# One two-bank transpose, a later channel mix and moved adds of x in a phase-mixing kernel on one Trainium2 core

## The chip, the cores and the metric

The kernel runs on one core of one Trainium2 chip. The metric is the device time in microseconds (us), and the median of several runs stands for a kernel. A single execution is also profiled: every instruction on every engine, every DMA transfer and the TensorE clock that was granted. TensorE multiplies matrices (PE in the profile; PEld is the loading of its weights), VectorE is DVE, ScalarE is ACT, GpSimd is POOL, and SP is the engine that issues most of the plain DMAs here.

## The reference

With B = 8, S = 4224, D = 192, the kernel computes a short causal convolution of x and then a token-mixing layer on the result:

```python
# convolution over 7 tokens, one softmax-normalised set of taps per head
out = np.einsum('hk,bskhg->bshg', w, x_unf)
x = out.reshape(B, S, D)
# mixing layer
theta = x @ w_theta
zr, zi = x * np.cos(theta), x * np.sin(theta)
y = np.einsum('ts,bsd->btd', w_tok_r, zr) + np.einsum('ts,bsd->btd', w_tok_i, zi)
u = x + y
return u + np.maximum(u @ w_ch, 0.0)
```

The two products with the 4224 x 4224 matrices w_tok_r and w_tok_i are nearly all of the arithmetic.

## The kernel before

**Tiling.** The source tokens are cut into 33 chunks of 128 (`NK`), the target tokens into 33 blocks of 128. All 8 batches lie side by side, so that a chunk of x is a tile of 128 tokens by 1536 values (`N`), in two halves of 768 (`GC`, four batches each). Only 11 chunks (`NW`) are held in SBUF at once. The work is a list of 58 steps (`NSTEP`). A step adds the contribution of the chunks that are held (up to 11) to two target blocks (`tbs`), so 17 steps (`NU`) go once round the targets, and each target block is visited three or four times. Between visits its partial sum `pv` lies in DRAM, in one of two arrays `part`: `load_rows` (line 356) fetches it one step ahead, and the end of `mix` (line 440) stores it.

**A step.** `mix` (line 414) computes a two-block step with seven runs of 2 x 11 matmuls of 384 columns (line 427) in place of eight, Strassen's scheme: some runs use sums of weight tiles. Each run ends with `give` (line 384), which adds its PSUM tile `y` into `pv`: on DVE (line 392), or on ACT in the first visit (line 390). The next step's weights are made while a step runs: `load_w` (line 307) fetches the raw rows on the POOL queue into `st`, `turn` (line 325) transposes them in 32 x 32 blocks on DVE (line 327), and `wsum` (line 333) forms the sums S1 to S4 on DVE (line 339, two fp16 inputs from SBUF).

**A chunk.** `Chunk` loads x (`xw`). `conv` makes the convolution (`pc`, line 200), evacuates it to the fp16 tile `x` and stores it in the DRAM array `xs`. `transpose` brings each half onto the other axis: six transposes into one bank of a PSUM tile `tp` (line 160), evacuated by `evacuate` to the tile `xT` (of the name `uT`; ACT line 148, DVE line 146). `theta` mixes the channels (`channel_mix`, PSUM tile `v`, line 138) and takes two sines on ACT (line 240), the first with a bias; `product` and `sums` (lines 245, 251) finish on DVE. The tiles `pc`, `tp` and `v` all come from `banks`: one pool of two buffers of two banks each. The first 11 chunks are made in the loop at the end of the program, where `between(n)` lets n pieces of the steps through; the other 22 are made inside steps 17 to 22 and 35 to 40.

**Adding x.** The sum u = x + y needs x in `pv`. `add_x` (line 368) does this once for each target block, in one of two ways. For 24 blocks it fetches x from `xs` into the one buffer `xr` and adds on POOL (line 374). For the 9 blocks of the last five steps (`late`) it lets a DMA on the POOL queue add `xs` into `part` in DRAM (line 379, two DMAs per block). That is four steps before they are needed, in steps 49 to 53.

**The output.** The last visit of a block (`final`, steps 41 to 57) ends with u. `cast` makes an fp16 copy `ub` on ACT (line 449); `cross_u` transposes it with a DMA through the crossbar, issued by ACT (line 155), in the 12 full final steps 41 to 52, and `turn_u` does so on PE in the last five; `output` mixes the channels (line 138 again), adds the relu to `pv` on DVE (line 464) and stores the result (line 469).

**Order.** `pe`, `dve`, `act` and `pool` chain the instructions of an engine in the order in which the program records them. That order is written by hand: each task of a step has a place between 0 and 7 (a run of matmuls is 1 unit, 3.6 us where 11 chunks are held), and `outputs` gives places in the list's own microseconds, 24.9 to a full step. An engine can start a recorded task as soon as its inputs are there, so a place binds PE, which is never far ahead, and is only an order for the others. The DMAs of SP are not chained; a scheduler orders them.

Of the kernel before, what the change touches and what calls it, by code (L numbers as in the profile page):

```python
# [9 lines left out]
AT = mybir.ActivationFunctionType  # L10
# [6 lines left out]
def kernel(  # L17
# [53 lines left out]
        mybir.DependencyClass.NoSync, mybir.DependencyReason.DATA  # L71
    )
# [84 lines left out]
    def transposed(uT, u, by_dve=False):  # L157
        tp = banks("tp", F16)
        for k in range(6):
            pe(nc.tensor.transpose(  # L160
                tp[:, 0, k * P : (k + 1) * P], u[:, k * P : (k + 1) * P], ident
            ))
        evacuate(uT.rearrange("p k s -> p (k s)"), tp[:, 0, 0 : 6 * P], by_dve)
# [3 lines left out]
    class Chunk:  # L167
# [53 lines left out]
        def transpose(self, g):  # L221
            if g == 0:
                self.xT = turned()
            transposed(
                self.xT[:, 6 * g : 6 * g + 6, :], self.x[:, g * GC : (g + 1) * GC],
                0 < self.k < 3 or (self.k, g) == (0, 1),
            )
# [27 lines left out]
        def tasks(self):  # L255

            for j in range(2):
                yield lambda j=j: self.conv(j)
            for g in range(NG):
                yield lambda g=g: self.transpose(g)  # L260
            for g in range(NG):
                yield lambda g=g: self.theta(g)
            yield lambda: self.product(Z11)
            yield lambda: self.product(Z21)
            yield lambda: self.sums(0)
            yield lambda: self.sums(1)
# [13 lines left out]
    class Step:  # L280


        def __init__(self, t):
            self.t, self.u, self.ks = t, unit(t), active(t)
            self.n = len(self.ks)
            self.tbs = [tb for tb in (2 * self.u, 2 * self.u + 1) if tb < NT]
            self.pair = len(self.tbs) == 2
            self.first = t < NU
            self.final = t + NU >= NSTEP
            self.late = self.final and self.n < NW  # L290
            self.ahead = self.late or 0 <= t + NU - NSTEP < 2
            visits = [v for v in range(NU, NSTEP) if v % NU == t % NU]
            self.adds = []
            for i, tb in enumerate(self.tbs):
                at = [v for v in visits if self.known(tb) < v - 1 and v + NU < NSTEP
                      and NU + 1 + base[-1] < v <= 2 * NU]
                at = at[0] if at else visits[-1]
                if t == at:
                    self.adds.append(i)
            self.time = 0.324 * self.n * (7 if self.pair else 4)  # L300
            self.st, self.w, self.ub, self.uT, self.pv = {}, {}, {}, {}, []
# [65 lines left out]

        def add_x(self, i):

            rows = slice(self.tbs[i] * P, (self.tbs[i] + 1) * P)  # L370
            if not self.ahead:
                xr = wk.tile([P, N], F16, name="xr", tag="xr", bufs=1)
                nc.sync.dma_start(out=xr, in_=xs[rows, :])
                pool(nc.gpsimd.tensor_tensor(  # L374
                    out=self.pv[i], in0=self.pv[i], in1=xr, op=ALU.add
                ))
                return
            for cols in (slice(0, HN), slice(HN, N)):
                pool(nc.gpsimd.dma_start(
                    out=part[(self.t // NU - 1) % 2][self.tbs[i], :, cols],  # L380
                    in_=xs[rows, cols], accum_op=ALU.add,
                ))
# [61 lines left out]
        def cast(self, i, g):  # L444
            if g == 0:
                self.ub[i] = wk.tile([P, N], F16, name="ub", tag="ub", bufs=2)
                self.uT[i] = turned()
            cols = slice(g * GC, (g + 1) * GC)
            act(nc.scalar.activation(  # L449
                out=self.ub[i][:, cols], in_=self.pv[i][:, cols], func=AT.Copy  # L450
            ))

        def turn_u(self, i, g):
            transposed(
                self.uT[i][:, 6 * g : 6 * g + 6, :], self.ub[i][:, g * GC : (g + 1) * GC]
            )
# [17 lines left out]
        def outputs(self):  # L474

            found = []
            for i in range(len(self.tbs)):
                if not self.late:
                    at = (4 if i else 0.9 - self.time / 7) if self.pair else 0.7
                    for g in range(NG):  # L480
                        found.append((at + g, lambda i=i, g=g: self.cast(i, g)))
                        found.append((at + 10.5 + 2.8 * g,
# [18 lines left out]
    def step_events(t):  # L501
        found = []
        s = steps[t]
        if t + 1 < NSTEP:
            found += steps[t + 1].w_tasks()
            found.append((1.6, steps[t + 1].load_rows))
            if not steps[t + 1].ahead:
                for i in steps[t + 1].adds:
                    found.append((3.3 + 1.7 * i, lambda i=i: steps[t + 1].add_x(i)))
        for s in steps[t:]:  # L510
            if s.ahead and t == s.t - (4 if s.late else 10):
                for i in s.adds:
                    found.append((3.3 + 1.7 * i, lambda s=s, i=i: s.add_x(i)))
# [8 lines left out]
        if t >= NU - 2:  # L522
# [4 lines left out]
            for k in (k for k in range(NK) if start[k] == t + 1 and k >= NW):  # L527
                pos = [0, .5, 1.3, 1.6, 2.1, 2.5, 3.1, 3.15, 3.4, 3.6]
# [116 lines left out]
    for i in range(NW + 2):  # L645
# [28 lines left out]
        if ch:  # L674
            ch.transpose(0)
        if old:
            old.product(Z11)
        between(1)
        if ch:
            ch.transpose(1)  # L680
# [9 lines left out]
    nc.vector.memset(wch[:, 1:3, :], 0.0)  # L690
# [36 lines left out]
```

## Time and profile before

| what | us |
| --- | --- |
| median of 13 runs | 1475.89 |
| fastest and slowest run | 1462.62, 1481.54 |
| the profiled execution, own time | 1477.95 |
| its span in the profile | 1476.2 |
| PE busy | 1425.0 (97%) |
| DVE busy | 1012.1 (69%) |
| ACT busy | 323.1 (22%) |
| POOL busy | 434.8 (29%) |

The profiled execution lies 2.1 us above the median, and 1.7 us of its time lie outside its span. PE's busy time says when it had a matmul in flight, not that it worked at its peak.

### The profile page before, as it was taken

The page shows a single profiled execution, that of the slowest core. Times are in us where ns is not written, and L with a number is a line of the kernel's source. Part 1 is how long each engine was busy: PE and PEld are TensorE (multiplying, and loading weights), DVE is VectorE, ACT ScalarE, POOL GpSimd, SP SyncE. Part 2 cuts the span into 40 slices and gives each one's busy share as a digit, 9 for nine tenths or more (in the row PEclk, how much of TensorE's full clock was granted, in tenths as well). Part 3 has the DMA queues.
Part 4 walks back from the last instruction along what each step waited for, and adds up shares of the span by engine and source line. Part 5 has one row for each costly group of instructions (what it writes and reads, how often), then busy time and mean ns, then how long its engine had stood idle before and what let it go on. Part 6 is the DMA issues. An engine that isn't in the chain of part 4 may idle for free.

```text
span 1476.2 us, 23773 instructions
## 1 busy us (share of the span) xinstructions
PE 1425.0 (97%) x9807; PEld 889.6 (60%) x9807; DVE 1012.1 (69%) x1050; ACT 323.1 (22%) x413; POOL 434.8 (29%) x655
## 2 busy tenths in 40 slices
PE   7889999999999999999999999999999999998997
PEld 4556666666666666666656566666666666555565
DVE  6884555545458687867767758768777786675575
ACT  6861111111134353000000005245001001000034
POOL 7422211111223322522413333332132133333210
PEclk9999999999999999999999999999999999999999
DMA  9976756464699999997978799999899989999983
GB/s 169 215 175 148 141 97 151 90 150 91 153 226 213 227 222 262 192 251 162 246 164 217 171 195 240 191 235 267 150 216 214 196 195 230 200 210 198 232 215 122
DMA packets 272028, 281.98 MB, mean 191 GB/s; under 512 B 106672, under 2 KB 240176, under 8 KB 271920
## 3 DMA queue, kind: packets, MB, share of 16 engines
q0 software_dynamic: 162464, 92.15, 48.3%
q1 hardware_dynamic: 71824, 178.88, 35.2%
q10 hardware_dynamic: 37632, 9.44, 4.2%
q8 instruction: 77, 1.26, 0.3%
q14 instruction: 31, 0.25, 0.1%
HBM read 245.49 MB, written 108.13 MB: 240 GB/s over the span
## 4 chain that ended last, share of the span: by engine, by line
PE 84%; DMA 6%; DVE 5%; ACT 3%; issue 1%; ACTq 0%; SPq 0%; DVEq 0%
PE y L427 75%; PE v L138 5%; DMA uT<-ub 4%; PE pc L200 2%; ACT z L240 1%; DVE wt L339 1%; DVE pv L392 1%; PE tp L160 1%; DMA pv<-part 1%; ACT uT L148 1%; DVE pv L464 1%; DVE wt L327 1%; DVE z L251 1%; DVE z L245 0%; DMA out_dram<-pv 0%
## 5 line engine op out<-in xcount | busy, mean ns | idle before, releaser
L427 PE MATMUL y<-z,wt 128*128 128x384 f16 x7656 | 1294.7, 327 | 11.7 <-DVE pv L392 10.8
L427 PEld LDWEIGHTS <-wt 128*128 128x128 f16 x7656 | 741.7, 98 | 489.6 <-issue 16.9
L392 DVE TENSOR_TENSOR pv<-y,pv 128x768 f32<-128x768 f32 x324 | 308.5, 953 | 310.5 <-PE y L427 271.2
L327 DVE STREAM_TRANSPOSE wt<-st 128x1408 f16<-128x1408 f16 (+7 forms) x224 | 327.6, 1465 | 41.5 <-PE y L427 36.2
L314 POOL DMA_DIRECT2D st<-in_moe_w_tok_i_dram x232 | 132.4, 579 | 500.7 <-DVE wt L327 485.3
L314 POOL DMA_DIRECT2D st<-in_moe_w_tok_r_dram x232 | 132.6, 580 | 460.4 <-DVE wt L327 447.1
L339 DVE TENSOR_TENSOR wt<-wt 128x1408 f16<-128x1408 f16 (+7 forms) x216 | 213.0, 986 | 45.6 <-PE y L427 43.4
L148 ACT ACTIVATE z<-pc 128x768 f16<-128x768 f32 x65 | 52.9, 813 | 389.4 <-PE pc L200 389.4
L449 ACT ACTIVATE ub<-pv 128x768 f16<-128x768 f32 x66 | 52.5, 836 | 361.3 <-DVE pv L392 332.4
L390 ACT ACTIVATE pv<-y 128x768 f32<-128x768 f32 x66 | 53.7, 813 | 282.7 <-PE y L427 282.7
L138 PEld LDWEIGHTS <-uT 128*128 128x128 f16 x1056 | 91.5, 99 | 38.8 <-DMA uT<-ub 15.6
L464 DVE SCALAR_TENSOR_TENSOR pv<-v,pv 128x768 f32<-128x768 f32 x66 | 62.8, 954 | 35.9 <-PE v L138 33.9
L187 POOL DMA_DIRECT2D xw<-in_x_dram x132 | 76.1, 585 | 30.8 <-issue 9.8
L374 POOL TENSOR_TENSOR pv<-pv,xr 128x1536 f32<-128x1536 f32 x24 | 74.8, 3118 | 13.4 <-issue 9.7
L148 ACT ACTIVATE uT<-tp 128x768 f16<-128x768 f16 x79 | 63.0, 815 | 63.1 <-PE tp L160 62.2
L251 DVE TENSOR_TENSOR z<-z 128x768 f16<-128x768 f16 x132 | 73.4, 556 | 3.8
L138 PE MATMUL v<-wch,uT 128*128 128x192 f16 x528 | 55.3, 249 | 15.0 <-DMA uT<-ub 13.1
L240 ACT ACTIVATE z<-v,half_pi 128x768 f16<-128x768 f32 x66 | 59.6, 903 | 42.9 <-PE v L138 42.7
L245 DVE TENSOR_TENSOR z<-z 128x1536 f16<-128x1536 f16 x66 | 60.4, 950 | 9.9 <-ACT z L240 9.9
L138 PE MATMUL v<-wth,uT 128*128 128x192 f16 x528 | 55.0, 248 | 3.0 <-ACT z L240 2.9
L240 ACT ACTIVATE z<-v 128x768 f16<-128x768 f32 x66 | 53.2, 805 | 0.0
L160 PE MATMUL tp<-ident,z 128*128 128x128 f16 x396 | 33.3, 221 | 8.4 <-ACT z L240 7.9
(43 smaller groups left out, 149.4 us busy)
## 6 DMA issues: line engine op xcount, KB each, us to landing
part<-pv SPq DMA_DIRECT2D x79, 768.0 KB, 4.2
pv<-part SPq DMA_DIRECT2D x79, 768.0 KB, 5.9
out_dram<-pv SPq DMA_DIRECT2D x66, 384.0 KB, 5.2
st<-in_moe_w_tok_r_dram POOLq DMA_DIRECT2D x136, 176.0 KB, 5.4
st<-in_moe_w_tok_i_dram POOLq DMA_DIRECT2D x136, 176.0 KB, 4.9
xs<-z SPq DMA_DIRECT2D x132, 96.0 KB, 4.5
xw<-in_x_dram POOLq DMA_DIRECT2D x121, 96.0 KB, 6.1
xr<-xs SPq DMA_DIRECT2D x24, 384.0 KB, 4.6
```

The source lines that it names most:

```text
L138: pe(nc.tensor.matmul(v[:, k, b * D : (b + 1) * D], lhsT=tT[:, 3 * k + b + i, :], rhs=w[:, 2 * b + i, :], start=(i == 0), stop=(i == 1),))
L148: act(nc.scalar.activation(out=out, in_=in_, func=AT.Copy))
L187: nc.gpsimd.dma_start(out=self.xw[lo : lo + n, h, :, :], in_=x[:, t0 : t0 + n, :].rearrange("b s d -> s b d"),)
L240: act(nc.scalar.activation(**args))
L251: dve(nc.vector.tensor_tensor(out=z[:, o, :], in0=z[:, a, :], in1=z[:, b, :], op=ALU.subtract))
L314: pool(nc.gpsimd.dma_start(out=st[a * Q : (a + 1) * Q, 0:nb, :, 0:n] .rearrange("i r bt s -> i (r bt) s"), in_=w[self.tbs[0] * P : (self.t ...
L327: dve(nc.vector.transpose(self.w[name][:, 0 : self.n, :, :], self.st[int(name[1])][:, int(name[0]) - 1, :, 0 : self.n * Q] .rearrange("p b ...
L339: dve(nc.vector.tensor_tensor(out=self.w[name][:, 0 : self.n, :, :], in0=self.w[a][:, 0 : self.n, :, :], in1=self.w[b][:, 0 : self.n, :, : ...
L374: pool(nc.gpsimd.tensor_tensor(out=self.pv[i], in0=self.pv[i], in1=xr, op=ALU.add))
L392: dve(nc.vector.tensor_tensor(out=o, in0=yv, in1=o, op=ALU.add))
L427: pe(nc.tensor.matmul(y[cn][:, q, 0:BH], lhsT=self.w[wn][:, c, :, :].rearrange("p bt i -> p (bt i)"), rhs=chunks[k].z[:, zn, q * BH : (q + ...
L464: dve(nc.vector.scalar_tensor_tensor(out=ub, in0=channel_mix(self.uT[i][:, 6 * g : 6 * g + 6, :], wch), scalar=0.0, in1=ub, op0=ALU.max, o ...
```

## The change

The diff has six edits.

1. `transposed` takes a list of halves. For x both halves go into the two banks of one PSUM tile, and one instruction evacuates 1536 columns. The first three chunks are evacuated by DVE, the rest by ACT. In the loop of the first chunks the 12 transposes stand together, ahead of the first product; in steps 17 to 22 and 35 to 40 the places of transposes and thetas move by about 0.1 unit.
2. In the full final steps `output` moves from the places 7.8, 10.6, 14.5, 17.3 (in the list's microseconds after the step's end) to 12, 14.7, 17.5, 20.2. The casts and the crossbar transfer of the second block move from 4, 5, 6 to 1, 2, 3.
3. The adds in DRAM for the last five steps move from steps 49 to 53 to steps 27, 29 and 31 (five blocks, in the other array `part`, one visit earlier) and step 41 (four blocks).
4. The fetch of `xr` is a task of its own (places 2 and 4). The POOL add moves from 3.3 and 5.0 to 3.6 and 5.6, and gets a wait: it starts after the DVE instruction recorded last before it has finished.
5. In the last two steps the first half of each cast is done by DVE instead of ACT.
6. The clearing of two slices of `wch` is chained in DVE's order.

```diff
@@ -70,6 +70,9 @@
     NOSYNC = mybir.DependencyInfo(
         mybir.DependencyClass.NoSync, mybir.DependencyReason.DATA
     )
+    SYNC = mybir.DependencyInfo(
+        mybir.DependencyClass.Sync, mybir.DependencyReason.SCHED_ONLY
+    )
     last = {}
 
     def in_order(engine, ins):
@@ -154,13 +157,20 @@
 
         act(nc.scalar.dma_start(out=uT, in_=u, transpose=True))
 
-    def transposed(uT, u, by_dve=False):
+    def transposed(uT, u, gs, by_dve=False):
+
         tp = banks("tp", F16)
-        for k in range(6):
-            pe(nc.tensor.transpose(
-                tp[:, 0, k * P : (k + 1) * P], u[:, k * P : (k + 1) * P], ident
-            ))
-        evacuate(uT.rearrange("p k s -> p (k s)"), tp[:, 0, 0 : 6 * P], by_dve)
+        for g in gs:
+            for k in range(6):
+                pe(nc.tensor.transpose(
+                    tp[:, g, k * P : (k + 1) * P],
+                    u[:, g * GC + k * P : g * GC + (k + 1) * P], ident,
+                ))
+        g = slice(gs[0], gs[-1] + 1)
+        evacuate(
+            uT[:, :, :].rearrange("p (g k) s -> p g (k s)", g=NG)[:, g, :],
+            tp[:, g, 0 : 6 * P], by_dve,
+        )
 
     Z11, T1, Z21, Z22, T2, T4, T3 = range(7)
 
@@ -218,13 +228,9 @@
                         out=xs[t0 : t0 + Q, :], in_=self.x[a * Q : (a + 1) * Q, :]
                     )
 
-        def transpose(self, g):
-            if g == 0:
-                self.xT = turned()
-            transposed(
-                self.xT[:, 6 * g : 6 * g + 6, :], self.x[:, g * GC : (g + 1) * GC],
-                0 < self.k < 3 or (self.k, g) == (0, 1),
-            )
+        def transpose(self):
+            self.xT = turned()
+            transposed(self.xT, self.x, range(NG), self.k < 3)
 
         def theta(self, g):
             v = channel_mix(self.xT[:, 6 * g : 6 * g + 6, :], wth).rearrange(
@@ -256,8 +262,7 @@
 
             for j in range(2):
                 yield lambda j=j: self.conv(j)
-            for g in range(NG):
-                yield lambda g=g: self.transpose(g)
+            yield self.transpose
             for g in range(NG):
                 yield lambda g=g: self.theta(g)
             yield lambda: self.product(Z11)
@@ -288,17 +293,21 @@
             self.first = t < NU
             self.final = t + NU >= NSTEP
             self.late = self.final and self.n < NW
-            self.ahead = self.late or 0 <= t + NU - NSTEP < 2
             visits = [v for v in range(NU, NSTEP) if v % NU == t % NU]
-            self.adds = []
+            quiet = [v for v in visits if start[2 * NW - 1] < v <= 2 * NU]
+            self.adds, self.ahead = [], []
             for i, tb in enumerate(self.tbs):
-                at = [v for v in visits if self.known(tb) < v - 1 and v + NU < NSTEP
-                      and NU + 1 + base[-1] < v <= 2 * NU]
-                at = at[0] if at else visits[-1]
-                if t == at:
+                known = self.known(tb)
+                if t not in ([v for v in quiet if known < v - 1] or visits[-1:])[:1]:
+                    continue
+                if not self.late:
                     self.adds.append(i)
+                else:
+                    far = known <= start[2 * NW - 1]
+                    self.ahead.append((i, 2 * NU - NW + 2 * (t % NU) if far else start[-1],
+                                       (t // NU - 1 - far) % 2))
             self.time = 0.324 * self.n * (7 if self.pair else 4)
-            self.st, self.w, self.ub, self.uT, self.pv = {}, {}, {}, {}, []
+            self.st, self.w, self.xr, self.ub, self.uT, self.pv = {}, {}, {}, {}, {}, []
 
         def known(self, tb):
 
@@ -365,20 +374,27 @@
                     )
                 self.pv.append(pv)
 
+        def load_x(self, i):
+            self.xr[i] = wk.tile([P, N], F16, name="xr", tag="xr", bufs=1)
+            nc.sync.dma_start(
+                out=self.xr[i], in_=xs[self.tbs[i] * P : (self.tbs[i] + 1) * P, :]
+            )
+
         def add_x(self, i):
 
-            rows = slice(self.tbs[i] * P, (self.tbs[i] + 1) * P)
-            if not self.ahead:
-                xr = wk.tile([P, N], F16, name="xr", tag="xr", bufs=1)
-                nc.sync.dma_start(out=xr, in_=xs[rows, :])
-                pool(nc.gpsimd.tensor_tensor(
-                    out=self.pv[i], in0=self.pv[i], in1=xr, op=ALU.add
-                ))
-                return
+
+            ins = pool(nc.gpsimd.tensor_tensor(
+                out=self.pv[i], in0=self.pv[i], in1=self.xr[i], op=ALU.add
+            ))
+            tc.add_manual_dep(ins.ins, last["dve"].ins.name, SYNC, reason="pace")
+
+        def add_ahead(self, i, which):
+
+            tb = self.tbs[i]
             for cols in (slice(0, HN), slice(HN, N)):
                 pool(nc.gpsimd.dma_start(
-                    out=part[(self.t // NU - 1) % 2][self.tbs[i], :, cols],
-                    in_=xs[rows, cols], accum_op=ALU.add,
+                    out=part[which][tb, :, cols], in_=xs[tb * P : (tb + 1) * P, cols],
+                    accum_op=ALU.add,
                 ))
 
         def give(self, y, i, h, copies):
@@ -446,14 +462,10 @@
                 self.ub[i] = wk.tile([P, N], F16, name="ub", tag="ub", bufs=2)
                 self.uT[i] = turned()
             cols = slice(g * GC, (g + 1) * GC)
-            act(nc.scalar.activation(
-                out=self.ub[i][:, cols], in_=self.pv[i][:, cols], func=AT.Copy
-            ))
+            evacuate(self.ub[i][:, cols], self.pv[i][:, cols], self.t >= NSTEP - 2 and g == 0)
 
         def turn_u(self, i, g):
-            transposed(
-                self.uT[i][:, 6 * g : 6 * g + 6, :], self.ub[i][:, g * GC : (g + 1) * GC]
-            )
+            transposed(self.uT[i], self.ub[i], [g])
 
         def cross_u(self, i):
             crossed(self.uT[i], self.ub[i])
@@ -476,10 +488,10 @@
             found = []
             for i in range(len(self.tbs)):
                 if not self.late:
-                    at = (4 if i else 0.9 - self.time / 7) if self.pair else 0.7
+                    at = 1 if i or not self.pair else 0.9 - self.time / 7
                     for g in range(NG):
                         found.append((at + g, lambda i=i, g=g: self.cast(i, g)))
-                        found.append((at + 10.5 + 2.8 * g,
+                        found.append((12 + 5.5 * i + 2.7 * g,
                                       lambda i=i, g=g: self.output(i, g)))
                     found.append((at + 2, lambda i=i: self.cross_u(i)))
                     continue
@@ -504,13 +516,12 @@
         if t + 1 < NSTEP:
             found += steps[t + 1].w_tasks()
             found.append((1.6, steps[t + 1].load_rows))
-            if not steps[t + 1].ahead:
-                for i in steps[t + 1].adds:
-                    found.append((3.3 + 1.7 * i, lambda i=i: steps[t + 1].add_x(i)))
-        for s in steps[t:]:
-            if s.ahead and t == s.t - (4 if s.late else 10):
-                for i in s.adds:
-                    found.append((3.3 + 1.7 * i, lambda s=s, i=i: s.add_x(i)))
+            for i in steps[t + 1].adds:
+                found.append((2 + 2 * i, lambda i=i: steps[t + 1].load_x(i)))
+                found.append((3.6 + 2 * i, lambda i=i: steps[t + 1].add_x(i)))
+        here = [(r, i, which) for r in steps for i, when, which in r.ahead if when == t]
+        for j, (r, i, which) in enumerate(here):
+            found.append((1.5 + 1.8 * j, lambda r=r, i=i, which=which: r.add_ahead(i, which)))
         if t + 2 < NSTEP:
             nxt = steps[t + 2]
             for m in (1, 2):
@@ -525,7 +536,7 @@
                 found.append((4.5, lambda k=k: load_chunk(k)))
             at = 0.1
             for k in (k for k in range(NK) if start[k] == t + 1 and k >= NW):
-                pos = [0, .5, 1.3, 1.6, 2.1, 2.5, 3.1, 3.15, 3.4, 3.6]
+                pos = [0, .5, 1.4, 2.2, 2.6, 3.1, 3.15, 3.4, 3.6]
 
                 def add(at, j, k):
                     def go():
@@ -672,12 +683,10 @@
             load_chunk(i + 3)
         between(1)
         if ch:
-            ch.transpose(0)
+            ch.transpose()
         if old:
             old.product(Z11)
-        between(1)
-        if ch:
-            ch.transpose(1)
+        between(2)
         if old:
             old.product(Z21)
         between(1)
@@ -687,7 +696,7 @@
         if old:
             old.sums(1)
         between(1)
-    nc.vector.memset(wch[:, 1:3, :], 0.0)
+    dve(nc.vector.memset(wch[:, 1:3, :], 0.0))
     for rows, i, part_w in channel_pieces(moe_w_ch):
         nc.gpsimd.dma_start(out=wch[rows, i, :], in_=part_w)
     ready[0] = NK
```

## The prediction

> **What bounds the kernel now.** I read the page first: its shares, its slices and the chain.
>
> ```profile
> span 1476.2 us, 23773 instructions
> PE 1425.0 (97%) x9807; PEld 889.6 (60%) x9807; DVE 1012.1 (69%) x1050; ACT 323.1 (22%) x413; POOL 434.8 (29%) x655
> ...
> PE 84%; DMA 6%; DVE 5%; ACT 3%; issue 1%; ACTq 0%; SPq 0%; DVEq 0%
> ```
>
> PE is the bound, and no edit here takes a matmul from it. What can be won is the time in which PE waits or runs slowly. So the next view is the list of waits, PE's rows alone:
>
> ```profile
> PE v L138 <- DMA uT<-ub: 13.1, 6, 3.1
> PE y L427 <- DVE pv L392: 10.8, 12, 1.8
> ...
> PE tp L160 <- ACT z L240: 7.9, 10, 1.1
> ```
>
> Each row has the total, the times and the longest. The first: the output's channel mix waits six times for the crossbar. The timeline shows where, here step 49's first block and, as a measure, the same 16 matmuls after a shorter wait:
>
> ```profile
> 1277.67 1.53 ACTq L155 DMA_TRANSPOSE uT<-ub  x1
> 1289.51 0.83 PE L138 MATMUL v<-wch,uT 128*128 128x192 f16 x8 [2.83 <-DMA uT<-ub]
> 1290.18 4.45 PE L427 MATMUL y<-z,wt 128*128 128x384 f16 x16
> ...
> 1320.97 2.76 PE L427 MATMUL y<-z,wt 128*128 128x384 f16 x16
> ```
>
> After the wait the 16 matmuls take 4.45 us, not 2.76. The windows view says why; its last three columns are granted clock, DMA share and GB/s:
>
> ```profile
> 1286.00:1290.00 4.00, 1.17 (x11) 0.69 (x9) 1.50 (x2) 0.00 (x0) 3.09 (x5) 1.00 1.13 192
> 1290.00:1294.00 4.00, 4.00 (x19) 2.01 (x17) 2.51 (x2) 0.00 (x0) 0.00 (x0) 0.57 1.56 158
> 1294.00:1298.00 4.00, 4.00 (x30) 2.69 (x29) 3.30 (x4) 0.00 (x0) 0.00 (x0) 1.00 1.13 292
> ```
>
> The wait itself had the full clock; the 4 us behind it had 0.57. Next, what ran beside these transfers, in the view of DMA issues (KB each, median us to landing):
>
> ```profile
> part<-xs POOLq DMA_DIRECT2D x18, 384.0 KB, 11.9
> ...
> uT<-ub ACTq DMA_TRANSPOSE x24, 6.7
> ```
>
> All 18 adds in DRAM are issued between 1259.7 and 1389.8 us. Five of the six waits lie there (1286 to 1368), and the transfers that PE waited for took 10.3 to 20.7 us from issue to landing. Of the earlier 16 transfers none took over 8.2 us, and one was waited for (0.65 us).
>
> **The change part by part.** (1) *Channel mix later, adds in DRAM elsewhere.* The six waits are 13.1 us. Slow matmuls follow four of them: 4.45 for 2.76 us (+1.7); at 1331 the mix in 1.18 for 0.82 and 18 matmuls in 4.46 for 3.09 (+1.7); at 1355 1.46 for 0.83 and 3.82 for 2.76 (+1.7); at 1368 4.77 for 3.09 (+1.7). That is 6.8 us, in sum 19.9 us. Here a rule of the Trainium skill stands against the row. TensorE: Matmul & The Clock Gate, Part 1, has the clock fall to half after at least one idle window of about 3.4 us. The longest wait here is 3.1 us, so by the rule no clock is lost and part 1 is worth 13.1 us. The row shows 0.57 behind a wait of 2.83 us, and the measurement decides: 19.9.
>
> Do the waits go? The first block's mix moves from 7.84 to 12 in the list's us. A full step lasts 27.7 us for 24.9 in the list, so that is 4.6 us. Its transfer had 7.6 us (1084.13 to 1091.73) to 9.0 us (1277.67 to 1286.68) before PE wanted it, and gets 12.2 to 13.6; the second block's mix moves by 3.3 us. These places alone just cover the contended first-block landings of 10.3 to 11.8 us. The adds, moved away, bring the landings to 8.2 us or less, so there are two covers, and I take the whole 19.9 (ends 10 and 19.9). The second block's earlier cast is only an order: ACT already did it 2 us into the step (1085.70), so the two transfers come no closer. Stores of the result move 3 us later and free `pv` later; the next fetch into that buffer stands 6.3 us into the following step and is used a step later. Its cover is some 20 us, its cost 0.
>
> The 18 moved DMAs cost POOL 1.0 us each, beside other work. In steps 27 to 31 and 41 they stand in POOL's queue behind the first weight fetch and ahead of the second, which needs 5 us to land and is used some 17 us after its issue. Two adds in a row (20.5 us at worst) leave a few us. Cost 0; if that cover is gone, three steps would each wait up to 5 us and lose 1.7 of clock: 20 us.
>
> (2) *POOL adds held back.* They disturb DVE, as in the timeline:
>
> ```profile
> 732.93 4.53 DVE L339 TENSOR_TENSOR wt<-wt 128x1408 f16<-128x1408 f16 x1
> 733.60 3.11 POOL L374 TENSOR_TENSOR pv<-pv,xr 128x1536 f32<-128x1536 f32 x1
> ...
> 738.95 0.91 DVE L392 TENSOR_TENSOR pv<-y,pv 128x768 f32<-128x768 f32 x1
> ...
> 739.92 2.27 PE L427 MATMUL y<-z,wt 128*128 128x384 f16 x13 [0.80 <-DVE pv L392]
> ```
>
> A weight sum beside an add takes 4.53 us for 0.88, the `give` behind it is late, and PE waits 0.80 and restarts. 13 of 24 adds stretch a sum so (2.4 to 4.6 us), but PE feels three, at 739, 815 and 841: 0.9 each, 2.8 in all. Held until S2 (or S4) is done, the 3.1 us add falls between the end of S2, near 3.7 units, and S4, past 5. There DVE has only `give`, turns and relu, which beside adds kept 0.96 and 1.63 us. Gain 2.8 (ends 0 and 2.8). The new wait holds POOL's queue; behind it stands the second weight fetch, which waits for the turn at 4.2 anyhow. The `give` of the next step waits for the add, at 2 units for the second block, whose add ends near 6.9: two units, 7 us, to spare.
>
> (3) *One transpose tile in the first chunks.* Second transposes wait for sines on ACT, because the pool has only two buffers:
>
> ```profile
> 76.98 1.55 ACT L148 ACTIVATE uT<-tp 128x768 f16<-128x768 f16 x2
> 77.19 0.49 PE L160 MATMUL tp<-ident,z 128*128 128x128 f16 x6 [0.66 <-ACT z L240]
> ```
>
> With one tile this wait, 7.9 us in ten places, moves to the next convolution, several matmuls further on. But then ACT is next: from 46.8 to 86.5 us (five chunks) it was busy 35.6 of 39.7. So at most 4.1 us can go there, plus what merging saves: two evacuations take 1.55, one of 1536 I put at 1.4 to 1.6. Before 46.8 the loads of x hold the pace. I take 3 (ends -1 and 7.9).
>
> (4) *The same tile in steps 17 to 22 and 35 to 40.*
>
> ```profile
> 430.34 0.50 PE L160 MATMUL tp<-ident,z 128*128 128x128 f16 x6
> ...
> 433.29 0.82 PE L138 MATMUL v<-wth,uT 128*128 128x192 f16 x8
> ```
>
> From transposes to theta are 2.95 us, and the new places keep 0.8 units, 3.0 us. Needed: 12 transposes 0.8, evacuation 1.5, hand-over 0.1: 2.4. Cost 0 for 20 chunks. Step 40 is short (a unit of some 2.4 us, so 1.9): two chunks late by 0.5, so -1 (ends 0 and -3).
>
> (5) *Casts in the last two steps.* Three casts of 0.83 us leave ACT, which was busy most of the last 12 us, for DVE, which waits for PE there. +1 (ends -1 and 2.5). (6) The `wch` clearing is 0.2 us on DVE, beside other work: 0.
>
> Sum: 19.9 + 2.8 + 3 - 1 + 1 = 25.7. From the span 1476.2 that leaves 1450.5, with the 1.7 outside 1452.2. This execution lies 2.1 above the median of the runs shown, and from the median the sum gives 1450.2. Between them: 1451.
>
> **The rivals.** *The transfers stay late* (0.14). If the crossbar is slow for another cause than the adds in DRAM, for instance the results' stores beside it, half of part 1 stays: 10 us, 1461. For it: the waits at 1091 and from 1286 to 1368 have such stores near. Against: 16 transfers without adds had stores beside them too and took at most 8.2 us.
>
> *The median has fewer of these waits* (0.12). The runs spread from 1462.6 to 1481.5, wider than anything but DMA timing explains. If the usual run has only the 13 us part or less, the gain is about 17: 1459.
>
> *The merged evacuation holds PE: slower* (0.05). Place: all 33 chunks, theta waiting for one evacuation of 1536 columns where the first half sufficed. The margin is 0.6 us of 3.0. If the evacuation takes 3.2 us rather than 1.5, PE loses about 1.0 per chunk, 33 us, against 25.7 won less 3 for part 3: 1486. It ends slower only from about 0.9 us per chunk. Against: ACT is idle there (1.84 us before its evacuation at 440.81), and 768 columns take 0.81.
>
> *The edits cancel* (0.05): part 1 falls short, and adds in DRAM delay weights: 1474.
>
> **How the numbers follow.** The likeliest case (0.64) is 1451, its own range 1442 to 1460 from parts 3 to 5. A measurement here can tell about 0.5%, 7.4 us, from no change: under 1468.5 is faster, over 1483.3 slower. Faster: 0.64 + 0.14 + 0.12 less what of them ends above 1468, 0.86; same 0.08 and slower 0.06, with the rest of the rivals. The range takes in the first two rivals and the whole of part 3: 1440 to 1468.
>
> **What would show it.** Right: no row of PE waiting for the crossbar over 1 us; clock 1.00 from 1240 us to the end of the full steps; no weight sum over 1 us; fewer transposes waiting for sines; the adds in DRAM near 700 to 770 and 1040 to 1065 us without a PE wait beside them. Wrong: PE waiting for `uT` on ACT or DVE before theta, a wait of POOL's weight fetches that reaches `turn`, or crossbar landings over 12 us without adds.

## The result: faster, and the crossbar waits are gone

| what | before | after |
| --- | --- | --- |
| median, us | 1477.82 (48 runs) | 1448.55 (11 runs) |
| ratio, 95% interval | | 0.9829 [0.9806, 0.9852] |
| fastest and slowest run, us | 1462.62, 2480.81 | 1447.64, 1456.25 |
| span of the profiled execution, us | 1476.2 | 1446.5 |
| clock of that execution | 0.994 | 0.998 |

The ratio and its interval are taken over fast executions alone, while the 48 runs and their median hold slower ones too. The gain is 29.3 us by these medians, 27.3 us from the median before that the prediction had, 29.7 us by the spans, and 25.2 us by the ratio (21.8 to 28.7 by its interval). The prediction said 1451. In what follows a kernel's gain is counted from the runs of before on the same chip, whose medians were 1474.0 to 1476.9 us.

The page of the changed kernel. The bound is the same, and in the chain DMA has fallen from 6% to 1%:

```profile
span 1446.5 us, 23748 instructions
PE 1416.3 (98%) x9809; PEld 887.9 (61%) x9809; DVE 979.0 (68%) x1051; ACT 315.5 (22%) x379; POOL 434.2 (30%) x655
...
PE 90%; DVE 4%; ACT 2%; POOL 1%; DMA 1%; issue 1%; DVEq 0%; SPq 0%; ACTq 0%; POOLq 0%
```

Next, PE's rows of its list of waits (total, times, longest). Lines have new numbers: 443 is the big run of matmuls, 408 `give` on DVE and 406 on ACT, 141 the channel mix, 151 the evacuation.

```profile
PE y L443 <- DVE pv L408: 7.5, 10, 2.5
PE v L141 <- ACT z L246: 3.0, 8, 0.6
PE y L443 <- ACT pv L406: 3.0, 3, 1.2
...
PE v L141 <- ACT uT L151: 2.1, 5, 0.8
```

The row that led the list of before (13.1 us for `uT` by the crossbar) is gone, and so is the one of second transposes waiting for sines (7.9 us). PE now waits three times for `give` on ACT in the first chunks (once before, 0.8 us), and five times for the evacuation before a theta (once before, 0.5 us). The windows view over the full final steps (the last three columns are granted clock, DMA share and GB/s) has PE busy throughout at full clock:

```profile
1270.00:1300.00 30.00, 30.00 (x203) 19.13 (x201) 21.54 (x21) 4.73 (x6) 4.54 (x8) 1.00 1.00 198
1300.00:1330.00 30.00, 30.00 (x202) 19.13 (x201) 21.33 (x21) 3.15 (x4) 10.78 (x10) 1.00 0.91 197
1330.00:1360.00 30.00, 30.00 (x203) 19.08 (x201) 20.06 (x23) 3.15 (x4) 6.86 (x12) 1.00 0.84 192
```

Where the gain lies can be read from PE alone. For each matmul I take the distance from its start to the next start, less the usual distance after a matmul of its kind, and add these up by stretches of the kernel:

| stretch | before, us | after, us | gain | prediction's part |
| --- | --- | --- | --- | --- |
| first chunks, to 111 us | 29.3 | 23.7 | 5.6 | (3) 3 |
| steps 17 to 22 | 4.3 | 3.6 | 0.7 | (4) 0 |
| POOL adds, 590 to 849 us | 2.2 | -0.7 | 2.9 | (2) 2.8 |
| steps 35 to 40 | 5.8 | 5.7 | 0.1 | (4) -1 |
| full final steps | 20.4 | -0.8 | 21.2 | (1) 19.9 |
| last five steps | 6.3 | 6.2 | 0.1 | (5) 1 |

A stretch without any wait gives about -0.1 per 37 us. The gains add up to 30.6 us, 0.9 more than the difference of the spans. Only 14 of the 24 POOL adds lie in the third stretch: the other ten run in the full final steps, between 1068 and 1322 us, and what they cost there is in that row.

The POOL adds now stand where they were to stand. This is the timeline after, at the place whose stretched sum cost PE a wait before:

```profile
732.62 3.10 POOL L386 TENSOR_TENSOR pv<-pv,xr 128x1536 f32<-128x1536 f32 x1 [1.32 <-DVE wt L348]
734.31 1.63 DVE L336 STREAM_TRANSPOSE wt<-st 128x1408 f16<-128x1408 f16 x1
...
737.01 0.96 DVE L408 TENSOR_TENSOR pv<-y,pv 128x768 f32<-128x768 f32 x1 [1.07 <-PE y L443]
737.88 0.88 DVE L348 TENSOR_TENSOR wt<-wt 128x1408 f16<-128x1408 f16 x1
```

The add waits for the sum ahead of it (`<-DVE wt L348`), runs beside a turn that keeps its 1.63 us, and is over when the next sum takes its 0.88. The group of these sums went from a mean of 1176 ns to the first row here; the second is the merged evacuation, 1.46 us for 1536 columns where two of 768 took 1.51 or more:

```profile
L348 DVE TENSOR_TENSOR wt<-wt 128x1408 f16<-128x1408 f16 x136 | 122.9, 904 | 35.3 <-PE y L443 33.8
...
L151 ACT ACTIVATE uT<-tp 128x1536 f16<-128x1536 f16 x30 | 43.8, 1458 | 51.8 <-PE tp L165 51.8
```

Step 40 shows the loss that was forecast, two thetas late. The bracket is the idle time ahead; from start to start the delay is 0.47 us each:

```profile
1008.78 0.83 PE L141 MATMUL v<-wth,uT 128*128 128x192 f16 x8 [0.30 <-ACT uT L151]
...
1016.98 0.83 PE L141 MATMUL v<-wth,uT 128*128 128x192 f16 x8 [0.30 <-ACT uT L151]
```

### The profile page after: what moved, and what is told of

It reads as the page before. It is cut to its first block, busy times and chain, and to the rows that moved or that the text cites. A ratio compares the mean times of both kernels' runs of the same rounds, so it can differ in the third digit from the quotient of the medians.

```text
span 1446.5 us, 23748 instructions
## 1 busy us (share of the span) xinstructions
PE 1416.3 (98%) x9809; PEld 887.9 (61%) x9809; DVE 979.0 (68%) x1051; ACT 315.5 (22%) x379; POOL 434.2 (30%) x655
## 4 chain that ended last, share of the span: by engine, by line
PE 90%; DVE 4%; ACT 2%; POOL 1%; DMA 1%; issue 1%; DVEq 0%; SPq 0%; ACTq 0%; POOLq 0%
PE y L443 82%; PE v L141 5%; PE pc L210 1%; PE tp L165 1%; ACT z L246 1%; DVE pv L408 1%; DVE z L257 1%; DVE z L251 1%; POOL st L323 1%; DVE wt L348 1%; DMA xw<-in_x_dram 1%; DVE wt L336 1%; DMA xs<-z 1%; DVE pv L476 0%; POOL xw L197 0%
## 5 line engine op out<-in xcount | busy, mean ns | idle before, releaser
L443 PE MATMUL y<-z,wt 128*128 128x384 f16 x7656 | 1283.6, 326 | 10.6 <-DVE pv L408 7.5
L443 PEld LDWEIGHTS <-wt 128*128 128x128 f16 x7656 | 740.8, 98 | 488.6 <-issue 10.6
L348 DVE TENSOR_TENSOR wt<-wt 128x1408 f16<-128x1408 f16 (+7 forms) x216 | 176.0, 815 | 40.7 <-PE y L443 38.2
L151 ACT ACTIVATE uT<-tp 128x1536 f16<-128x1536 f16 (+1 forms) x48 | 58.2, 1216 | 74.4 <-PE tp L165 74.4
L210 PE MATMUL pc<-xw,bands 96*64 96x192 f16 x528 | 35.8, 258 | 2.6 <-ACT bands L625 1.1
```

The costliest lines, as they stand in the source:

```text
L151: act(nc.scalar.activation(out=out, in_=in_, func=AT.Copy))
L348: dve(nc.vector.tensor_tensor(out=self.w[name][:, 0 : self.n, :, :], in0=self.w[a][:, 0 : self.n, :, :], in1=self.w[b][:, 0 : self.n, :, : ...
L443: pe(nc.tensor.matmul(y[cn][:, q, 0:BH], lhsT=self.w[wn][:, c, :, :].rearrange("p bt i -> p (bt i)"), rhs=chunks[k].z[:, zn, q * BH : (q + ...
```

## The experiments

Three sets of runs. The first undoes parts of the change on the changed kernel; the last does parts of it alone, on the kernel before; between them stands a measurement of the clock. The theory was the prediction's: crossbar transfers come late because the adds in DRAM run beside them, a late one costs its wait and a stretch of half clock, and either of two covers (mixes placed later, adds elsewhere) is enough. The rival was that the median lost less there than the profiled execution, and that the gain came from elsewhere.

**The changed kernel again,** beside its variants on the same chip (no edit).

> The changed kernel again, beside the next three, as their common measure. Expected 1448 us, ratio to the kernel before 0.98; no wait of PE for the crossbar, granted clock 1.00 in the full final steps.

Measured: 1448.9 us (1447.68 to 1451.1), ratio 0.9837 [0.981, 0.9864], no wait for the crossbar. It is the measure for the next three.

**Part 1 undone,** both its halves:

```diff
-    at = 1 if i or not self.pair else 0.9 - self.time / 7
+    at = (4 if i else 0.9 - self.time / 7) if self.pair else 0.7
...
-    found.append((12 + 5.5 * i + 2.7 * g,
+    found.append((at + 10.5 + 2.8 * g,
...
-    self.ahead.append((i, 2 * NU - NW + 2 * (t % NU) if far else start[-1],
-                       (t // NU - 1 - far) % 2))
+    self.ahead.append((i, t - 4, (t // NU - 1) % 2))
...
-    found.append((1.5 + 1.8 * j, lambda r=r, i=i, which=which: r.add_ahead(i, which)))
+    found.append((3.3 + 1.7 * i, lambda r=r, i=i, which=which: r.add_ahead(i, which)))
```

> The changed kernel with the old places of cast, crossbar transfer and channel mix and the old steps 49 to 53 for the adds in DRAM; the other edits stay. My theory (the waits for the crossbar and the slow clock behind them are 19.9 us of the gain, whatever the other edits do): 1448 + 20 = 1468 us, five or six waits of PE between 1230 and 1350 us, clock near 0.6 behind those over 2.5 us. Rival (the median has fewer of these waits than the profiled run): 1456 to 1460. Rival (most of the gain comes from the other edits): under 1453.

Measured: 1455.51 us (1453.54 to 1461.13), 6.6 over the changed kernel and not 20. Its profiled execution (span 1459.4), the slowest of the six, has one wait for the crossbar. In its timeline the adds at 1263 and 1278 lie around the two transfers, which took 20.4 us each to land, and the windows view has the clock at half behind the wait:

```profile
1268.21 1.29 ACTq L158 DMA_TRANSPOSE uT<-ub  x1
...
1288.71 1.46 PE L141 MATMUL v<-wch,uT 128*128 128x192 f16 x8 [11.48 <-DMA uT<-ub]
1289.80 0.31 PEld L441 LDWEIGHTS <-wt 128*128 128x128 f16 x2
1289.96 2.35 PE L441 MATMUL y<-z,wt 128*128 128x384 f16 x9
```

```profile
1288.00:1292.00 4.00, 3.29 (x17) 2.25 (x18) 1.72 (x2) 0.00 (x0) 0.00 (x0) 0.57 1.29 193
1292.00:1296.00 4.00, 4.00 (x30) 2.70 (x29) 3.30 (x4) 0.00 (x0) 0.00 (x0) 1.00 1.17 255
```

The other 22 transfers landed in 3.2 to 9.0 us, six of them among adds in DRAM, and none was waited for. So the mechanism is there, but on this base it strikes once, where the kernel before had six waits. Either part 1 is worth 6.6 us, or the other edits had already taken some of its stalls. The third set bears on this.

**Each half undone by itself:** the first two lines of that diff (places old, adds moved), then the last two (places new, adds in steps 49 to 53).

> Only the places of cast, transfer and mix are the old ones; the adds in DRAM stay in steps 27 to 31 and 41. Theory (without adds beside them the transfers land in about 8 us, and the old place gave 7.6 to 9.0): 1449 to 1453 us, a few waits under 1 us, no fall of the clock. Rival (the place is what matters; the changed kernel's own transfers take up to 9 us, and 11 beside step 41's adds): waits of 1 to 4 us in several steps, 1455 or more.

> Only the adds in DRAM are back in steps 49 to 53; mixes stay late. Theory (the new places give 12.2 to 13.6 us to the first block and the old contended first-block transfers took 10.3 to 11.8, so the places alone just suffice): 1449 to 1452 us, transfers of 10 to 20 us, at most one or two short waits. Rival (places and adds are both needed): two or three waits over 2 us with a slow clock behind, 1456 to 1460.

Measured: 1450.97 us with the old places, +2.1; 1449.33 with the old adds, +0.4. With the old places the profile has one wait, in step 41, whose own adds in DRAM now run beside its transfers:

```profile
1044.68 3.51 POOL L395 DMA_DIRECT2D part<-xs  x4
1048.26 1.39 ACTq L158 DMA_TRANSPOSE uT<-ub  x1
...
1058.54 0.83 PE L141 MATMUL v<-wch,uT 128*128 128x192 f16 x8 [1.22 <-DMA uT<-ub]
```

With the old adds there is none, though transfers took up to 9.6 us. Each cover alone is enough but for that one wait.

**Parts 3, 2 and 5 undone,** one each. Two transpose tiles again; the wait of the POOL add taken out; the casts back on ACT:

```diff
-            yield self.transpose
+            for g in range(NG):
+                yield lambda g=g: self.transpose(g)
...
-                pos = [0, .5, 1.4, 2.2, 2.6, 3.1, 3.15, 3.4, 3.6]
+                pos = [0, .5, 1.3, 1.6, 2.1, 2.5, 3.1, 3.15, 3.4, 3.6]
...
-            tc.add_manual_dep(ins.ins, last["dve"].ins.name, SYNC, reason="pace")
...
-            evacuate(self.ub[i][:, cols], self.pv[i][:, cols], self.t >= NSTEP - 2 and g == 0)
+            evacuate(self.ub[i][:, cols], self.pv[i][:, cols])
```

> The changed kernel with x transposed half by half again: two tiles, two evacuations, the old places and the old split between DVE and ACT. My theory (the merged tile takes PE's waits for sines in the first 11 chunks and costs about 1 us in step 40): 1448 + 3 to 5 us, 1452, ten waits of the second transposes for the sines of about 0.8 us each. Rival (ACT or the loads of x hold the pace of the first chunks anyway): 1448 to 1449.

> The changed kernel without the wait of the POOL add for DVE; its new place and the earlier fetch of xr stay. Theory (the wait keeps the adds off the weight sums): weight sums of up to 4.5 us again, two to four PE waits of 0.9 us behind late adds of y, 1448 + 3 = 1451. Rival (the place in POOL's order alone does it): 1448, hardly any sum over 1 us.

> The changed kernel with all casts on ACT. Theory: the last 20 us are 1 us longer, 1449 to 1450, within what can be measured of the changed kernel. Rival (DVE is as full as ACT there): no difference or a shorter end.

Measured, on another chip than the four above, so the differences to 1448.9 are good to 1 us at best: two tiles 1453.64 (+4.7), no wait of the POOL add 1452.72 (+3.8), casts on ACT 1450.28 (+1.4). With two tiles the waits of transposes for sines are back in the list:

```profile
PE tp L165 <- ACT z L247: 8.3, 10, 1.1
```

and PE's excess in the first chunks is 29.2 us, as it was before the change. Without the wait of the POOL add the stretched sums are back in the timeline (here the add runs from 729.76, and the two sums take 5.38 us together where 1.76 is usual):

```profile
729.76 4.38 POOL L386 TENSOR_TENSOR pv<-pv,xr 128x1536 f32<-128x1536 f32 x1
730.45 5.38 DVE L348 TENSOR_TENSOR wt<-wt 128x1408 f16<-128x1408 f16 x2
```

PE felt two of them in that execution, 1.8 us; it was the fastest of the six. The casts can't be told from nothing: the excess in the last stretch is 6.2 us with them on ACT and on DVE.

**The clock by itself.** Bursts of 60 of the same matmuls, with PE made to wait for a chain of DVE instructions between them; nothing of the reference is computed.

```python
for rep in range(10):
    for m in (64, 640, 896, 1152, 1408, 1664, 1920, 2400, 3000):
        # 60 matmuls of 128 x 384, then DVE works on m columns; the next burst waits for it
```

> Nothing of the reference is computed: bursts of 60 matmuls of 384 columns alternate with pauses in which PE waits for DVE, nine lengths from about 1 to 5 us, ten times each; the output is set to zero. It measures the disputed price of a wait. My reading of the profile (waits of 2.6 to 3.1 us were followed by about 4 us at half clock, 1.3 us by none): the half clock appears behind pauses from about 2 to 2.6 us on and costs 1.7 us each. Rival (the page's window of 3.4 us of idle, free-running): none below 3.4 us. A window that need only be mostly idle would give some falls between the two, not every time.

The timeline of PE (start, duration, count, and in brackets the idle time ahead), where a burst at full clock takes 9.92 us:

```profile
39.72 9.92 PE L31 MATMUL y<-z,w 128*128 128x384 f16 x60 [1.71 <-DVE w L39]
51.61 9.92 PE L31 MATMUL y<-z,w 128*128 128x384 f16 x60 [1.97 <-DVE w L39]
63.78 11.51 PE L31 MATMUL y<-z,w 128*128 128x384 f16 x60 [2.24 <-DVE w L39]
77.79 9.92 PE L31 MATMUL y<-z,w 128*128 128x384 f16 x60 [2.50 <-DVE w L39]
90.49 11.60 PE L31 MATMUL y<-z,w 128*128 128x384 f16 x60 [2.77 <-DVE w L39]
105.56 12.79 PE L31 MATMUL y<-z,w 128*128 128x384 f16 x60 [3.47 <-DVE w L39]
122.44 12.88 PE L31 MATMUL y<-z,w 128*128 128x384 f16 x60 [4.09 <-DVE w L39]
```

Over the ten rounds no burst was slow after 0.84, 1.44 or 1.71 us; 1 of 10 was after 1.97, 8 after 2.24, 5 after 2.50, 7 after 2.77, all ten after 3.47, and all nine after 4.09. A slow burst lost 1.4 to 1.7 us after waits up to 2.77, and 1.3 to 3.0 after longer ones. So waits of 2 to 3 us can cost half clock, as the kernel before showed, and not each of them does.

Which of them does is not chance. In the trace's record of the granted clock every stretch of half clock in these bursts begins on a fixed grid of 3.41 us and lasts one or two of its intervals. In the kernel before they begin at 1290.43, 1331.39, 1355.29 and 1368.94 us: 12, 7 and 4 such intervals apart. Here are the intervals around the 2.24 us and the 2.50 us wait above, in the windows view (PE busy follows the length, the granted clock is third from the end):

```profile
60.22:63.63 3.41, 1.32 (x9) 0.59 (x6) 1.99 (x3) 0.00 (x0) 1.00 1.03 317
63.63:67.04 3.41, 3.26 (x11) 1.58 (x12) 0.09 (x1) 0.00 (x0) 0.50 1.03 321
73.87:77.28 3.41, 1.42 (x9) 0.64 (x7) 1.92 (x2) 0.00 (x0) 1.00 1.03 319
77.28:80.70 3.42, 2.91 (x18) 1.78 (x19) 0.42 (x2) 0.00 (x0) 1.00 1.03 320
```

The shorter wait left PE idle for 2.09 us of one interval, and the next had half clock. The longer one lies across a border, so its first interval has 1.99 us of idle time and its second 0.51, and no half clock follows. Of the 293 intervals at full clock in these bursts, the 39 with more than 2.005 us of idle time were all followed by half clock; of the 254 others one was (1.97 us). This limit holds for these bursts: in the kernel before, an interval with 1.80 us of idle time, at 37.7 us, was followed by half clock too. So the third reading of the expectation came true: the interval need only be mostly idle. An interval at half clock loses at most half of 3.41 us, the 1.7 us seen behind each of the four waits in the kernel before.

**Each part alone.** Now the other way round: of the change only part 1; only part 2; only part 3; and of part 1 only the later places. Each is made by putting the undo edits above together, so that all the rest is as before, but for three edits that all four kernels keep: the fetch of `xr` as a task of its own, the places 3.6 and 5.6 of the POOL adds, and the chained clearing of `wch`. What these three do by themselves was not run.

> Part 1 alone: new places of the casts, transfers and mixes and the DRAM adds in steps 27 to 31 and 41; two transpose tiles, POOL adds without the wait for DVE, and casts on ACT as before. The prediction's theory (part 1 is worth its 19.9 us whatever else is in the kernel): 19 to 20 us under before. Theory of the undo runs (part 1 is worth 6.6 us, and the usual run of before waits less for the crossbar than the profiled one): 5 to 8 us under before. Interplay (without the wait of the POOL adds the transfers lose more): between, 12 to 18 us. No wait of PE for the crossbar over 1.5 us in any of the three.

> The later mixes alone (places of casts, transfers and mixes new), the DRAM adds in steps 49 to 53 as before, and parts 2, 3 and 5 undone. If one cover suffices on the kernel before too, as the undo runs showed on the kernel after: the same time as part 1 alone within 1 us, and no wait for the crossbar. If the contention is harder without the wait of the POOL adds: some waits of 1 to 3 us beside the DRAM adds, 3 to 10 us over part 1 alone.

> Part 2 alone: the POOL adds wait for DVE, all else as before, the DRAM adds beside the output's transfers. The prediction: 2.8 us under before. The undo runs: 3.8 us. Interplay (stretched weight sums shift PE, POOL and ACT against each other, so that transfers and DRAM adds meet more often): 8 to 13 us, with fewer waits for the crossbar than the six of before.

> Part 3 alone: one transpose tile with one evacuation, all else as before. The prediction: 3 us under before in the first chunks, 2 with the loss in step 40. The undo runs: 4.7 us. Interplay (an earlier end of the first chunks shifts later transfers): 8 to 12 us, with fewer or shorter waits for the crossbar.

| kernel | median, us | runs, us | ratio, 95% interval | under before |
| --- | --- | --- | --- | --- |
| before, same chip | 1476.88 | 1465.5 to 1484.6 (17) | | |
| part 1 alone | 1455.46 | 1453.8 to 1455.7 (5) | 0.9853 [0.9808, 0.9897] | 21.4 |
| its places alone | 1456.14 | 1455.6 to 1457.4 (5) | 0.986 [0.9815, 0.9905] | 20.7 |
| part 2 alone | 1458.53 | 1455.7 to 1471.8 (6) | 0.9886 [0.9838, 0.9935] | 18.4 |
| part 3 alone | 1463.66 | 1458.4 to 1476.7 (12) | 0.993 [0.9896, 0.9963] | 13.2 |

Part 1, together with the three shared edits, is worth 21.4 us, near the 19.9 that the prediction gave it, and its interval, 15 to 28 us, leaves out both the 6.6 of the undo and the 13.1 of the waits without the clock. No wait for the crossbar is left in it nor in the places alone, which have the adds in DRAM still beside the transfers. So the later places are enough to end the waits.

But the kernels with part 2 and part 3 alone gain 18.4 and 13.2 us, far more than the stalls of these parts. These are their waits for the crossbar, first with part 2 alone, from the timeline, then with part 3 alone, from the list of waits:

```profile
1282.09 0.83 PE L141 MATMUL v<-wch,uT 128*128 128x192 f16 x8 [0.88 <-DMA uT<-ub]
1310.84 0.83 PE L141 MATMUL v<-wch,uT 128*128 128x192 f16 x8 [0.91 <-DMA uT<-ub]
1342.01 0.83 PE L141 MATMUL v<-wch,uT 128*128 128x192 f16 x8 [3.27 <-DMA uT<-ub]
```

```profile
PE v L141 <- DMA uT<-ub: 4.3, 5, 1.1
```

Three waits and five, 5.1 and 4.3 us, in place of six with 13.1; and where none passes 1.1 us, no clock is lost behind them either. Part 3's profiled execution is the fastest of its twelve runs, so the usual one waits more. The excess of PE says where these gains lie. In the full final steps it is 20.4 us before, -0.5 with part 1 alone, -0.8 with its places alone, 6.6 with part 2 alone and 5.1 with part 3 alone. So the kernels with parts 2 and 3 gained 13.8 and 15.3 us in a stretch where part 3 has no edit at all. The three gains add up to 53.0 us, where the whole change has 25 to 29: they overlap in the waits for the crossbar, which can be removed once.

Two things can make this overlap, and the runs do not tell how much is due to each. First, the three shared edits count in every one of these gains, and the undo of part 1 keeps them too. Two of them move fetches and POOL adds that lie in the full final steps as well. Part 3's own stretch, the first chunks, gained about 5 us in its profile, so up to about 8 of its 13.2 us can be theirs (an estimate), and part 1 would then be worth as much less than 21.4. Second, the wait of part 2 acts in the full final steps too. In three of these steps before, and in four with part 3 alone, a POOL add stretches a weight sum, the first block's transfer is issued late, and PE wants it 7.4 to 7.6 us after its issue, in place of 8.8 to 9.1. The first wait of before, at 1092 us, and two of part 3 alone, at 1088 and 1201 us, follow transfers with 7.6 us. With part 2 alone all twelve first blocks have 8.9 to 9.1 us.

The waits from 1280 us on are not explained by this, since their first-block transfers had 9.0 to 9.1 us. Nor by the distance between adds and transfers: in the profiles of before, of part 1 undone, of part 2 and of part 3 alone, the first contended transfer is issued 4.9 to 5.0 us after an add (1272.7 and 1277.7 before), and it landed in 11.8, 20.4, 9.9 and 10.0 us. With the same distance the landing varies twofold between these kernels, and the runs of one kernel vary too. The kernels with one cover or both spread by 2 to 6 us over five or six runs (the changed kernel's 11 runs by 9 us); those with the old places and the old adds by 8 to 29 us, over 6 to 17 runs.

## Why the prediction was right

**Part 1, 19.9 us: right in mechanism, and in size for the whole change.** The stretch of the full final steps gives 21.2 us, and its waits and half clock are gone. How much of that is due to part 1's own edits is open: 21.4 us together with the shared edits, 6.6 us by the undo. The rows of half clock, which the prediction counted against the rule of the Trainium skill (TensorE: Matmul & The Clock Gate, Part 1), are borne out by the measurement of the clock: waits of 2.24 us, under the page's 3.4, brought it 8 times in 10. The record's 3.41 us is the length of an interval; about 2.0 us of idle time within one was enough. By the rule as the prediction read it the sum would have been 6.8 us smaller, 1458. The two covers, each just sufficient, are shown by undoing each (+2.1 and +0.4 us). What the step did not see is that its stalls are not its own: with the other edits in place, undoing it costs 6.6 us. For the sum of the whole change this made no difference.

**A transfer's need was set too low.** The prediction had landings of 8.2 us or less once the adds are away. After the change, transfers with no add beside them took up to 9.2 us, and the two of step 41, among its four blocks' adds, 11.1 and 11.3:

```profile
part<-xs POOLq DMA_DIRECT2D x18, 384.0 KB, 9.4
uT<-ub ACTq DMA_TRANSPOSE x24, 6.9
```

The slack, 13.1 us for every first block (12.2 to 13.6 by the forecast), held all of them. With the old places 10.2 us in step 41 was too late. In that step only the later places were cover enough.

**Part 2, 2.8 us: right for the adds it looked at.** The profile gives 2.9 and the undo 3.8; sums beside adds are what it removes. That late sums in the full final steps also delay the crossbar transfers, as shown above, it did not see. The forecast "no weight sum over 1 us" failed in two places (1.62 us at 592 and 2.63 at 612), which PE did not feel.

**Part 3, 3 us: the term that was too small.** The table gives 5.6 and the undo 4.7. The cap of 4.1 us, the room on ACT over five chunks from 46.8 to 86.5 us, held for what it covered: added up one by one, the distances over 0.15 us lose 3.7 there. ACT did become the next limit (busy 36.0 of 38.3 us from 44.6 on), and new waits for `give` on ACT came, as forecast. What failed is the range of the term: the rest of the 5.6 us, 1.9, lies ahead of 46.8 and behind 86.5, where it had put nothing, and 3 was taken below the cap itself. This rest is not firm: in the eight profiles with one tile the middle loses 5.0 to 5.1 us (8.5 to 8.8 with two tiles), while the whole stretch varies from 21.4 to 24.8 (29.2 to 29.4 with two). That the loads hold the pace at first was right: to 37 us the excess is 10.1 us before and 10.4 after.

**Parts 4 and 5, -1 and +1: both about 0.** The two late thetas of step 40 came as forecast, 0.47 us each between starts, but other waits in these steps became shorter. The last stretch has 6.3 us before and 6.2 after: the casts on ACT were not what held it.

**The rivals.** *The transfers stay late* fell: with the adds moved and the places and stores old, the 22 transfers away from adds landed in 3.3 to 8.5 us. *The median has fewer of these waits* fell with the result: by the medians on the same chip the gain is 25.8 us, not 17. *The merged evacuation holds PE* fell: it takes 1.46 us, and the theta of 20 of the 22 later chunks does not wait for it. *The edits cancel* fell: PE has no wait beside the moved adds.

The prediction lies 2.4 us over the measured median. Against the table its sum is 4.9 us short: 2.6 in part 3, 1.3 in part 1, 1.8 in part 4 and 0.1 in part 2, less 0.9 too much in part 5. The profiled executions lie 29.7 us apart, and the medians that the prediction compared 27.3; that this hides part of the shortfall is luck.

## What to carry to other kernels

A wait for a DMA whose landing varies should be given more than the usual landing: with the later places, and the three shared edits, the time fell by 20.7 us and the spread of the runs from 19 us to 2, with the adds in DRAM still beside the transfers. Do each part alone as well as undo it: where parts alone add up to twice the whole, they overlap, and neither the undo of one (6.6 us here) nor its gain alone (21.4) is what it is worth. And run what is left over when all parts are undone: without it, that remainder counts in every part. To the length of a wait on TensorE belongs the half clock behind it, here half as much again.

## What the runs showed of the hardware that was not expected

Half clock came and went on a fixed grid of 3.41 us, in the bursts and in the kernel before. In the bursts it came when PE had been idle for more than about 2.0 us within one interval. So an idle time of 1.97 us brought it in one case of ten and one of 2.24 us in eight of ten, by where it fell on the grid, at 1.4 to 1.7 us a time. A crossbar transfer of one 128 x 1536 fp16 tile landed in 3.2 us at best and in 20.7 at worst, and at the same distance behind an add in DRAM in 9.9 us in one kernel's profile and 20.4 in another's.
